# Attention in front of two feed-forward layers: scores of the first two pairs regrouped, score banks in two tiles, selectors made pair by pair

## The chip, the cores and the metric

The kernel runs on one core of one Trainium2 chip. Its engines work at the same time and wait for one another by semaphores: TensorE (PE in the profile, with its weight loads as PEld), VectorE (DVE), ScalarE (ACT), GpSimd (POOL), and SyncE (SP), which here only issues DMAs. The metric is the time on the device in microseconds (us), from launch to end. Three runs of the kernel before took 990.05, 990.08 and 991.07 us, median 990.08.

## The reference

Three stages follow one another; the data are float32.

```python
scores = scale * np.matmul(q, k.transpose(0, 1, 3, 2))          # 4 x 8 heads, 576 x 576, head size 64
cum = np.cumsum(np.log(np.clip(f, 0.0001, 1.0)), axis=-1)
scores = np.where(causal, -1e9, scores + cum[:, :, :, None] - cum[:, :, None, :])
attn = np.exp(scores - np.max(scores, axis=-1, keepdims=True))
x = np.matmul(attn / (np.sum(attn, axis=-1, keepdims=True) + 1e-09), v)
h = x @ w_in;  x = (h * np.cos(h)) @ w_out                      # layer one: 2304 x 512 -> 2048 -> 512
g = x @ w_gate; x = (g / (1 + np.exp(-g)) * (x @ w_val)) @ w_out2   # layer two: 512 -> 1536 -> 512
```

## The kernel before

**Pairs and steps.** Attention works on 16 pairs of heads; a pair fills the 128 rows of TensorE with twice 64. For one pair the score matrix falls into five row tiles, written 0 to 4; tile t < 4 has 128 rows and 128 (t + 1) columns for each head, tile 4 holds the last 64 rows of both heads. The steps have one letter and a tile: `S` computes scores on TensorE (`emit_s`, L381), `M` adds the mask and takes the row maximum on VectorE (L415), `E` is the exponential with row sums on ScalarE (L423), `T` transposes on TensorE (L461), `C` copies the transposed tile out of PSUM (L483 and L485: `C10` and `C11` on VectorE, the others on ScalarE), `V` multiplies with v on TensorE (L513), `N` multiplies with the reciprocal sums on VectorE (L522). The reciprocals go their own way: `ra` on GpSimd (L433), `rb` on VectorE (L435), `rt` a transpose on TensorE (L438), `rc` a copy on ScalarE (`row`, L441), `rd` a write to DRAM, `re` and `rf` two reads that spread it over the rows (L451). `q` splits q and k into a rounded high part and a low rest on GpSimd (xqh L111, xql L108); a score is then three products (high x high, low x high, high x low) in fp32r and a fourth one that adds the decay: a selector (sel) times the cumulative logarithms (cs). Pair 0 is not split; its scores are one fp32 product and the decay. `qb` fills for tile 4 block-diagonal tiles (bd, h for high, l for low, s for the selector) from q and from selr, a small input.

**What sets the order.** The string `SCH` (L46) lists the steps of one iteration; `M21@2` in iteration n is step M, tile 2, second head, of pair n - 2. `in_order` (L586) holds each engine to that order. An iteration has parts of pairs n down to n - 5. In the steady state TensorE goes through T20 (end of the string), T40, rt, T30, T10, T11, T00, T01 of one pair, S4 and S1 of the next, V1 and V0 of an older one, then S3, S2, S0 of the pair after.

**Buffers.** All scores lie in one PSUM tile `s` of four banks (L348); `SAT` gives tiles 1 and 3 the first bank of each head, 0, 2 and 4 the second. Everything that TensorE makes else in this stage takes one of four PSUM tiles `t` in turn, ten times in an iteration: T20, T40, rt, T30, T10, T11, T00, T01, V1, V0. Each take waits until the one four places before it is read out. So T10 waits for C20, T11 for C40, T00 for rc, T01 for C30. Filler matmuls (`warm`, L323) keep TensorE going; `WAIT` (L538) puts five of them behind steps of pairs 0 and 1.

**The beginning.** f lands, VectorE clips it, ScalarE takes the logarithm, VectorE sums it up in two halves of 288 columns (L337 to L342). ScalarE makes the selectors of all 16 pairs (sel, L335 and L343).

**Behind attention.** Layer one (L627 on) multiplies with fp32r halves of weights and data: L246 into h, then ScalarE and VectorE make n, r, the sine, gh and gl, and L660 multiplies gh and gl with w_out. Its tiles n, r (pool mp2) and gh, gl (mp3) are laid where attention had its tiles. The sine table of ScalarE is loaded at L606, after the last `E`. The first matmuls of layer one stand between the last transposes and V steps on TensorE.

Of the kernel before, what the change touches and what calls it, by code (L numbers as in the profile page):

```python
# [26 lines left out]
CH = 384  # L27
# [18 lines left out]
SCH = "M21@2 ld@0 M00@2 T40@3 M01@2 rt@3 M30@2 T30@3 re@4 C40@3 C30@3 rc@3 T10@3 M31@2 w6@4 C10@3 w1@3 T11@3 C11@3 T00@3 C00@3 T01@3 E20@2 C01@3 S4@2 S1@2 V1@4 rf@4 E21@2 w2@3 E30@2 w3@3 w4@3 E31@2 q3@1 M40@2 M10@2 wd@2 E00@2 E01@2 q0@0 M11@2 rd@3 V0@4 S3@1 lv@3 E40@2 S2@1 w5@3 E10@2 xk@3 xo@5 E11@2 q1@0 qb@0 S0@1 T20@2 N1@4 ra@2 N0@4 rb@2 M20@1 w7@4 C20@2 q2@0"  # L46
# [44 lines left out]
def body(ctx: ExitStack, tc: tile.TileContext, qk, v, f, w_in, w_out, w_gate, w_val, w_out2, mask_c, ident_c, sel_c, out):  # L91
# [211 lines left out]
    bd = [[ap1.tile([128, 128], F32R, name=f"bd{k}{a}") for a in "hls"] for k in range(2)]  # L303
# [5 lines left out]
    sel = aps.tile([128, NPAIR, 128], F32R, name="sel")  # L309
    POOL.memset(mask[:, 0:384], 0.0)  # L310
    POOL.memset(mask4[:, 0:512], 0.0)
    for b in (bd0, *bd[0], *bd[1]):
        POOL.memset(b.bitcast(F32), 0.0)
# [14 lines left out]
    warm(WARM, ones[:, 0:128], ones[:, 0:512])  # L328
    DVE.memset(hpi, float(np.pi / 2))
    ACT.activation(out=hpi[:, 0:1], in_=ones[:, 0:1], func=AF.Ln)  # L330
    ACT.activation(out=hpi[:, 0:1], in_=ones[:, 0:1], func=AF.Identity, scale=float(np.pi / 2))
    DVE.tensor_scalar(out=lf, in0=lf, scalar1=1e-4, scalar2=1.0, op0=ALU.max, op1=ALU.min)
    ACT.activation(out=lf, in_=lf, func=AF.Ln)
    for k in range(2):
        ACT.copy(out=sel[:, k], in_=selr[:, k:k + 1].to_broadcast([128, 128]))  # L335
    for a, b in ((0, S // 2), (S // 2, S)):
        DVE.tensor_tensor_scan(out=cum[:, a:b], data0=ones[:, a:b], data1=lf[:, a:b], initial=cum[:, a - 1:a] if a else 0.0,  # L337
                               op0=ALU.mult, op1=ALU.add)
        hi = lc[:, S + a:S + b]
        DVE.tensor_copy(hi.bitcast(F32R), cum[:, a:b])  # L340

        DVE.scalar_tensor_tensor(out=cs[:, a:b], in0=hi, scalar=selr[:, NPAIR:NPAIR + 1], in1=cum[:, a:b], op0=ALU.mult, op1=ALU.add)  # L342
    ACT.copy(out=sel[:, 2:], in_=selr[:, 2:NPAIR, None].to_broadcast([128, NPAIR - 2, 128]))  # L343

    for t in P4s:
        DVE.memset(t[:, S:], 0.0)

    sall = ps_s.tile([128, 2, 2, 512], F32, name="s")  # L348

    SAT = {0: (1, 384), 1: (0, 0), 2: (1, 0), 3: (0, 0)}  # L350
# [3 lines left out]
    def emit_q(i, k):  # L354

        if k == 0:
            xq[i] = [aps.tile([128, 2, S], F32R, tag=a, name=a, bufs=2) for a in ("xqh", "xql")]
        (h, l), x = xq[i], raws[i]
        if k % 2 == 0:
            pool_round(h[:, k // 2], x[:, k // 2])  # L360
        else:
            subtract(POOL, l[:, k // 2], x[:, k // 2], h[:, k // 2])
# [18 lines left out]
    def emit_s(i, t):  # L381
        p = s_parts(i)
        if t < 4:
            q0, ext, _ = QT[t]
            bank, lo = SAT[t]
            o = sall[:, :, bank, lo:lo + ext]
            for m, (x, y) in enumerate(p):
                for e in range(2):
                    b = slice(64 * e, 64 * e + 64)
                    PE.matmul(o[:, e], lhsT=x[b, 0, q0:q0 + 128], rhs=y[b, 1, :ext], start=(m == 0), stop=False)  # L390
            for e in range(2):
                b = slice(64 * e, 64 * e + 64)
# [83 lines left out]
    def emit_c(i, g, e):  # L476
# [61 lines left out]
    WAIT = {("S0", 0): 1, ("S1", 0): 2, ("S1", 1): 2}  # L538

    def op(o, i):  # L540

        if not 0 <= i < NPAIR:
            return
        k, e = o[0], int(o[-1]) if o[-1] in "01" else 0
# [5 lines left out]
        elif k == "S":  # L550
            emit_s(i, int(o[1]))
# [489 lines left out]
```

## Time and profile before

| | |
|---|---|
| median of three runs | 990.08 us |
| time of the profiled execution | 988.04 us |
| its span, first to last instruction | 986.3 us |
| TensorE busy | 973.1 us, 99% of the span |
| VectorE, ScalarE, GpSimd busy | 721.9, 495.2, 476.7 us |
| granted clock of TensorE, mean | 0.998 of full speed |

The profiled execution took 1.74 us more than its span and 2.04 us less than the median of the runs. A busy share in the profile holds overlapped stretches of matmuls whose ends are modelled, so a TensorE that shows no idle time may still lose some; weight loads (PEld) show such small gaps. From about 190 us to the end the kernel is in layers one and two.

### The profile page before, as it was taken

What the parts mean: (1) busy time and instruction counts of PE and PEld (TensorE: products, weight loads), DVE (VectorE), ACT (ScalarE), POOL (GpSimd) and SP (SyncE); (2) the same over time, 40 slices, a digit from 0 to 9 for tenths busy, and PEclk for the clock granted to TensorE, in tenths of its full rate; (3) what the DMA queues carried; (4) which work ended last, traced back from release to release, by engine and by line L of the source; (5) the groups of instructions that cost most, each with busy time, mean ns of one, the idle gap of its engine ahead of it and who ended that gap; (6) DMA issues with size and microseconds to landing.
All of it is one profiled execution on the core that took longest, in us unless ns stands there. A gap on an engine that the chain in (4) does not pass through costs nothing.

```text
span 986.3 us, 18039 instructions
## 1 busy us (share of the span) xinstructions
PE 973.1 (99%) x6458; PEld 930.6 (94%) x6458; DVE 721.9 (73%) x1297; ACT 495.2 (50%) x1112; POOL 476.7 (48%) x531
## 2 busy tenths in 40 slices
PE   8999999899999999999999999999999999999998
PEld 5787877799999999999999999999999999999998
DVE  5888888587788878778785636756768585977874
ACT  5878788455545556556554532323224132443432
POOL 6787875442238678677593004455445455300000
PEclk9999999999999999999999999999999999999999
DMA  4666665433547877769767773325941329954331
GB/s 159 205 187 202 214 182 174 137 107 118 167 150 232 263 224 246 245 210 289 245 198 244 251 272 113 95 82 186 345 128 49 117 73 393 334 161 144 117 105 43
DMA packets 108697, 182.61 MB, mean 185 GB/s; under 512 B 8880, under 2 KB 72256, under 8 KB 108608
## 3 DMA queue, kind: packets, MB, share of 16 engines
q1 hardware_dynamic: 108608, 181.46, 56.8%
q8 instruction: 51, 0.84, 0.4%
q14 instruction: 38, 0.31, 0.1%
HBM read 118.43 MB, written 62.99 MB: 184 GB/s over the span
## 4 chain that ended last, share of the span: by engine, by line
PE 93%; ACT 4%; DMA 1%; issue 1%; DVE 0%; ACTq 0%
PE h L246 20%; PE t L660 19%; PE b L844 11%; PE c L844 8%; PE a L844 8%; PE b L903 6%; PE c L903 4%; PE a L903 4%; PE t L513 4%; PE s L390 3%; ACT pt L485 3%; PE t L461 2%; PE t L663 2%; PE s L399 2%; ACT P L423 1%; PE s L393 1%
## 5 line engine op out<-in xcount | busy, mean ns | idle before, releaser
L246 PE MATMUL h<-xh,w 128*128 128x384 f32 x768 | 149.5, 335 | 0.0
L660 PE MATMUL t<-gh,w 128*128 128x384 f32 x704 | 136.3, 334 | 2.0 <-ACT gh L645 2.0
L246 PEld LDWEIGHTS h<-xh,w 128*128 128x128 f32 x768 | 134.4, 188 | 0.4 <-POOL w L108 0.2
L815 POOL TENSOR_TENSOR s<-u,s 128x384 f32<-128x384 f32 x36 | 41.3, 1147 | 184.1 <-ACT s L814 171.4
L660 PEld LDWEIGHTS t<-gh,w 128*128 128x128 f32 x704 | 123.3, 188 | 2.3 <-ACT gh L645 2.3
L844 PE MATMUL b<-c,wu 128*128 128x384 f32 x648 | 121.1, 334 | 0.0
L637 ACT ACTIVATE n<-h 128x384 int32<-128x384 f32 x96 | 47.1, 491 | 144.9 <-PE h L246 134.0
L639 DVE SCALAR_TENSOR_TENSOR r<-h,n 128x384 f32<-128x384 f32 x96 | 53.4, 556 | 86.7 <-ACT n L637 86.4
L844 PEld LDWEIGHTS b<-c,wu 128*128 128x128 f32 x648 | 113.1, 188 | 0.1
L246 PE MATMUL h<-xl,w 128*128 128x384 f32 x384 | 82.0, 334 | 0.0
L844 PE MATMUL c<-c,wu 128*128 128x384 f32 x432 | 80.7, 334 | 0.0
L844 PE MATMUL a<-c,wu 128*128 128x384 f32 x432 | 80.7, 334 | 0.0
L725 DVE TENSOR_TENSOR u<-b,p 128x768 f32<-128x768 f32 (+1 forms) x54 | 41.9, 777 | 50.0 <-PE b L844 30.0
L844 PEld LDWEIGHTS a<-c,wu 128*128 128x128 f32 x432 | 75.4, 188 | 0.0
L844 PEld LDWEIGHTS c<-c,wu 128*128 128x128 f32 x432 | 75.4, 188 | 0.0
L660 PE MATMUL t<-gl,w 128*128 128x384 f32 x352 | 75.2, 334 | 0.0
L108 POOL TENSOR_TENSOR w<-ta,w 128x512 fp32r<-128x512 f32 x32 | 45.3, 1415 | 58.1 <-ACT w L183 30.1
L423 ACT ACTIVATE P<-P,mx 128x384 f32<-128x384 f32 (+3 forms) x128 | 70.6, 556 | 1.7 <-DVE mx L415 1.7
L246 PEld LDWEIGHTS h<-xl,w 128*128 128x128 f32 x384 | 67.9, 188 | 0.0
L641 ACT ACTIVATE r<-r,hpi 128x384 f32<-128x384 f32 x96 | 59.5, 620 | 12.7 <-DVE r L639 11.7
L169 DVE SCALAR_TENSOR_TENSOR ta<-wraw,ta 128x512 int32<-128x512 int32 x68 | 65.4, 961 | 0.4
L903 PE MATMUL b<-wu,c 128*128 128x256 f32 x486 | 62.8, 283 | 0.6 <-issue 0.6
(150 smaller groups left out, 2125.5 us busy)
## 6 DMA issues: line engine op xcount, KB each, us to landing
wu<-wu SPq DMA_DIRECT2D x63, 512.0 KB, 4.9
wraw<-in_w_out_dram SPq DMA_DIRECT2D x28, 512.0 KB, 4.1
wu<-hi SPq DMA_DIRECT2D x54, 256.0 KB, 3.5
gd<-g SPq DMA_DIRECT2D x72, 192.0 KB, 2.3
gt<-gd SPq DMA_DIRECT2D x36, 384.0 KB, 4.4
raw<-in_qk_dram SPq DMA_DIRECT2D x16, 576.0 KB, 5.3
wu<-sums SPq DMA_DIRECT2D x36, 256.0 KB, 3.6
xb<-x SPq DMA_DIRECT2D x24, 384.0 KB, 8.1
```

Source lines behind the costliest of these rows:

```text
L108: eng.tensor_tensor(out=o, in0=a, in1=b.bitcast(F32), op=ALU.subtract)
L169: DVE.scalar_tensor_tensor(out=ta, in0=hi, scalar=-(1 << 30), in1=ta, op0=ALU.bitwise_and, op1=ALU.bitwise_or)
L246: PE.matmul(ps, lhsT=w[:, a, 128 * kk:128 * kk + 128], rhs=b[:, kk], start=(n == 0), stop=(n == 3 * KD - 1))
L423: ACT.activation(out=o, in_=o, func=AF.Exp, scale=-1.0, bias=mxt[p % 8][:, t:t + 1], accum_out=smt[p // 2 % 3][:, c:c + 1])
L637: ACT.activation(out=n, in_=h, func=AF.Copy, scale=INV2PI, bias=0.25)
L639: DVE.scalar_tensor_tensor(out=r, in0=h, scalar=INV2PI, in1=n, op0=ALU.mult, op1=ALU.subtract)
L641: ACT.activation(out=r, in_=r, func=AF.Sin, bias=hpi, scale=float(2 * np.pi))
L660: PE.matmul(acc[m][:, :CH], lhsT=wo[:, q, 128 * m:128 * m + 128], rhs=x, start=(j == a and n == 0), stop=False)
L725: (e or DVE).tensor_tensor(out=o, in0=a, in1=b, op=op)
L815: e.tensor_tensor(out=s, in0=C[:, 0], in1=s, op=ALU.mult)
L844: PE.matmul(o[:, mem], lhsT=wu[q, i][1][:, mem, x, 128 * kt:128 * kt + 128], rhs=cmb[i][:, y, kt], start=bool(s and n == 0), stop=(n == 5) ...
L903: PE.matmul(ot, lhsT=cmb[i][:, x, q], rhs=wu[NQ + q // 2, i][1][:, q % 2, y], start=bool(s and n == 0), stop=(n == 3 * NQ - 1), skip_group ...
```

## The change

- **Pairs 0 and 1.** Pair 1 takes its tiles 0, 2 and 3 from the raw q and k in one fp32 product, as pair 0 does; its tiles 1 and 4 stay split in three. Pair 0 computes tile 1 right after tile 3, into two tiles `t`, and tile 4 last; its M40 comes after M10 and M11. Two `warm` matmuls remain of five.
- **Score banks.** `s` becomes two tiles, sA (tiles 0, 2, 4) and sB (1, 3). In the string, S2 and S0 now stand before S3; pair 1 alone keeps S3, S2, S0.
- **Order of the transposes.** rt stands before T40 on TensorE, and the copy rc right after C20 on ScalarE. The copies of tails (`tails`) take both heads in one instruction.
- **Selectors.** sel for 16 pairs goes. GpSimd fills, for each pair, one of three tiles of 128 x 256 (two instructions of 64 x 128, zeros in the middle), from which tiles 0 to 3 and tile 4 take their selector. bd holds h and l in one tile, so that one instruction fills both: four small instructions a pair in place of six. xqh and xql become one tile xq.
- **The beginning.** The logarithms go in halves of 384 and 192 columns through clip, logarithm, sum and rounding; the table of the exponential is loaded right behind the logarithms.
- **Sine table and layer one.** The sine table is loaded after the last C01. mp2 and mp3 are made after the tiles of the second chunk (xpool2) and of the sums (pp), and with `reuse_waits="tile"`.

```diff
-SCH = "M21@2 ld@0 M00@2 T40@3 M01@2 rt@3 ... C40@3 C30@3 rc@3 T10@3 ... S3@1 lv@3 E40@2 S2@1 w5@3 ... S0@1 T20@2 N1@4 ra@2 N0@4 rb@2 M20@1 w7@4 C20@2 q2@0"
+SCH = "M21@2 ld@0 M00@2 rt@3 M01@2 T40@3 ... C20@3 rc@3 C40@3 C30@3 T10@3 ... S2@1 lv@3 E40@2 S0@1 w5@3 ... S3@1 T20@2 N1@4 ra@2 N0@4 rb@2 M20@1 w7@4 q2@0"
...
+    bd = [ap1.tile([128, 2, 128], F32R, name=f"bd{k}") for k in range(2)]
+    sels = [ap1.tile([128, 256], F32R, name=f"sel{k}") for k in range(3)]
...
-    for k in range(2):
-        ACT.copy(out=sel[:, k], in_=selr[:, k:k + 1].to_broadcast([128, 128]))
...
+    for c in halves:
+        DVE.tensor_scalar(out=lf[:, c], in0=lf[:, c], scalar1=1e-4, scalar2=1.0, op0=ALU.max, op1=ALU.min)
+        ACT.activation(out=lf[:, c], in_=lf[:, c], func=AF.Ln)
+    ACT.activation(out=sinp, in_=ones[:, 0:1], func=AF.Exp)
...
-    sall = ps_s.tile([128, 2, 2, 512], F32, name="s")
+    sA, sB = (ps_s.tile([128, 2, 512], F32, name=n) for n in ("sA", "sB"))
...
     def emit_b(i):
         q = slice(512, S)
+        s = sels[i % 3]
         for e in range(2):
             b = slice(64 * e, 64 * e + 64)
-            pool_round(bd[i % 2][2][b, b], selr[b, i:i + 1].to_broadcast([64, 64]))
+            pool_round(s[b, 128 * e:128 * e + 128], selr[b, i:i + 1].to_broadcast([64, 128]))
+        for e in range(2):
+            b = slice(64 * e, 64 * e + 64)
             if i:
-                for o, x in zip(bd[i % 2], xq[i]):
-                    pool_round(o[b, b], x[b, 0, q].bitcast(F32))
+                pool_round(bd[i % 2][b, :, b], xq[i][b, :, 0, q].bitcast(F32))
...
+        if i > 1 or i == 1 and t in (1, 4):
+            xh, xl = xq[i][:, 0], xq[i][:, 1]
+            h, l = bd[i % 2][:, 0], bd[i % 2][:, 1]
+            p = (xh, xh, h), (xl, xh, l), (xh, xl, h)
+        else:
+            p = (raws[i], raws[i], bd0),
...
-    WAIT = {("S0", 0): 1, ("S1", 0): 2, ("S1", 1): 2}
+    WAIT = {("S3", 0): 2}
...
+        if i == 0:
+            o = {"M40": "M10", "M10": "M11", "M11": "M40"}.get(o, o)
+        elif i == 1:
+            o = {"S2": "S3", "S0": "S2", "S3": "S0"}.get(o, o)
...
-                    if len(after_e) == 9:
-                        ACT.activation(out=sinp, in_=hpi, func=AF.Sin)
+            if n - int(off) == NPAIR - 1 and o == "C01":
+                ACT.activation(out=sinp, in_=hpi, func=AF.Sin)
...
-    mp2 = lctx.enter_context(tc.tile_pool(name="mp2", bufs=1))
-    mp3 = lctx.enter_context(tc.tile_pool(name="mp3", bufs=3))
     xpools[1] = lctx.enter_context(tc.tile_pool(name="xpool2", bufs=1))
     pp = lctx.enter_context(tc.tile_pool(name="pp", bufs=1))
+    mp2 = lctx.enter_context(tc.tile_pool(name="mp2", bufs=1, reuse_waits="tile"))
+    mp3 = lctx.enter_context(tc.tile_pool(name="mp3", bufs=3, reuse_waits="tile"))
```

On TensorE at the start, before: raw is q and k of the pair, cs the cumulative logarithms, L326 a filler; x2 is one matmul for each head.

```order
L390 MATMUL s<-raw 128x512 [waits DMAHW1_49]
L390 MATMUL s<-raw 128x512
L393 MATMUL s<-cs,sel 128x512 [waits DVE_49,Activation_49]
L393 MATMUL s<-cs,sel 128x512
L390 MATMUL s<-raw 128x384 x2
L393 MATMUL s<-cs,sel 128x384 x2
L390 MATMUL s<-raw 128x128 x2
L393 MATMUL s<-cs,sel 128x128 x2
L326 MATMUL t<-mask,ident 128x448 [waits DMAHW6_49,DMAHW3_49,Pool_49]
L399 MATMUL s<-raw,bd_121 128x288 [waits DVE_49,Pool_49]
```

The same place on TensorE in the changed kernel:

```order
L400 MATMUL sA<-raw 128x384 [waits DMAHW1_49]
L400 MATMUL sA<-raw 128x384
L403 MATMUL sA<-cs,sel_117 128x384 [waits DVE_49,Pool_49]
L403 MATMUL sA<-cs,sel_117 128x384 [waits Pool_49]
L400 MATMUL sA<-raw 128x128 x2
L403 MATMUL sA<-cs,sel_117 128x128 x2
L400 MATMUL sB<-raw 128x512 x2
L403 MATMUL sB<-cs,sel_117 128x512 [waits DVE_49]
L403 MATMUL sB<-cs,sel_117 128x512
L400 MATMUL t<-raw 128x256 x2
L403 MATMUL t<-cs,sel_117 128x256 x2
...
L408 MATMUL sA<-raw,bd_120 128x288 [waits DVE_49,Pool_49]
```

The tile of 384 columns moved ahead of the one of 512, the one of 256 moved ahead of tile 4 (L408, before L399), and the selector is waited for on GpSimd and not on ScalarE.

On ScalarE, the copies of one pair behind its last exponentials, before (128x2x256 is C20, the two of 3x64 are C40, then C30 with two tails, row is the copy rc, L161 a step of the weights):

```order
L485 COPY pt<-t 128x2x256 [waits PE_49]
L485 COPY pt<-t 128x3x64 [waits PE_49]
L485 COPY pt<-t 128x3x64
L485 COPY pt<-t 128x2x128 [waits PE_49]
L485 COPY pt<-t 128x2x64 x2
L441 COPY row<-t 9x128
L161 ACTIVATE ta<-wraw 128x512 [waits DMAHW0_49]
```

The same copies in the changed kernel:

```order
L493 COPY pt<-t 128x2x256 [waits PE_49]
L449 COPY row<-t 9x128 [waits PE_49]
L493 COPY pt<-t 128x2x3x64 [waits PE_49]
L493 COPY pt<-t 128x2x128 [waits PE_49]
L493 COPY pt<-t 128x2x2x64
L161 ACTIVATE ta<-wraw 128x512 [waits DMAHW0_49]
```

The copy of the reciprocals moved from the sixth place behind C20 to the first, and six copies of tiles became four. On TensorE its transpose (rc_174, before rc_176) moved ahead of T40, whose tile is Q. Before:

```order
L461 MATMUL t<-ident,P_110 128x128 [waits Activation_49]
L461 MATMUL t<-ident,Q_113 128x128 [waits PE_49,Activation_49]
L461 MATMUL t<-ident,Q_113 128x128 x2
L438 MATMUL t<-ident,rc_176 9x128 [waits DVE_49,PE_49]
L461 MATMUL t<-ident,P_109 128x128 [waits PE_49]
```

and in the changed kernel:

```order
L469 MATMUL t<-ident,P_110 128x128 [waits Activation_49]
L446 MATMUL t<-ident,rc_174 9x128 [waits DVE_49]
L469 MATMUL t<-ident,Q_113 128x128 [waits PE_49,Activation_49]
L469 MATMUL t<-ident,Q_113 128x128 x2
L469 MATMUL t<-ident,P_109 128x128 [waits PE_49]
```

With this the tiles `t` are taken in the order T20, rt, T40, T30, T10, T11, T00, T01, so that T11 waits for rc and T00 for C40.

## Rows read from the trace of the kernel before

**Rows 1.** Busy time by stretch: engines' us (instructions), granted clock, DMA share, GB/s.
```profile
0.00:20.00 20.00, 15.24 (x62) 8.31 (x63) 8.51 (x30) 11.19 (x26) 13.48 (x37) 0.91 0.56 194
```

**Rows 2.** Waits from 20 to 160 us: us in total, times, longest.
```profile
PEld t L461 <- ACT pt L485: 4.4, 14, 0.4
```

**Rows 3.** Timeline of one pair's transposes: start, us, engine, line [idle before].
```profile
163.32 1.65 ACT L485 COPY pt<-t 128x512 f32<-128x512 f32 x6 [1.64 <-PE t L461]
163.45 0.27 PE L438 MATMUL t<-ident,rc 128*9 128x128 f32 x1
164.80 0.25 ACT L441 COPY row<-t 9x128 f32<-9x128 f32 x1
165.02 0.86 PEld L461 LDWEIGHTS t<-ident,P 128*128 128x128 f32 x8 [0.31 <-ACT pt L485]
165.87 0.51 PE L399 MATMUL s<-xqh,bd1h 128*128 128x288 f32 x2
167.77 2.93 PE L513 MATMUL t<-pt,vt 128*64 128x320 f32 x28
```

**Rows 4.** Timeline of the beginning.
```profile
7.97 0.50 PE L393 MATMUL s<-cs,sel 64*128 64x512 f32 x2 [1.19 <-DVE cs L342]
12.55 1.93 PE L399 MATMUL s<-raw,bd 128*128 128x288 f32 x4 [2.03 <-DVE mx L415]
17.01 0.24 POOL L111 TENSOR_SCALAR bd0l<-xql 64x64 fp32r<-64x64 f32 x1
19.27 0.25 POOL L433 TENSOR_SCALAR rc<-sm 128x9 f32<-128x9 f32 x1 [2.02 <-ACT P L423]
25.43 1.77 PE L326 MATMUL t<-mask,ident 128*128 128x448 f32 x4
```

**Rows 5.** Busy time by stretch, behind the wait at 12.55 us (columns as in Rows 1).
```profile
13.00:14.00 1.00, 1.00 (x5) 0.71 (x3) 0.00 (x0) 1.00 (x6) 1.00 (x2) 0.50 0.00 0
15.00:16.00 1.00, 1.00 (x6) 0.74 (x6) 0.00 (x0) 0.00 (x0) 1.00 (x3) 0.50 0.92 355
```

**Rows 6.** Groups by form on GpSimd, 0 to 160 us: busy us, mean ns.
```profile
L108 POOL TENSOR_TENSOR xql<-raw,xqh 128x576 fp32r<-128x576 f32 x30 | 42.5, 1416 | 1.4
L111 POOL TENSOR_SCALAR xqh<-raw 128x576 fp32r<-128x576 f32 x30 | 20.6, 687 | 25.6 <-PE s L390 25.3
L111 POOL TENSOR_SCALAR bd1s<-selr 64x64 fp32r<-64x64 f32 x16 | 6.9, 434 | 0.5
L111 POOL TENSOR_SCALAR bd1h<-xqh 64x64 fp32r<-64x64 f32 x16 | 3.8, 239 | 0.5
```

**Rows 7.** Timeline from the end of S1 of pair 1.
```profile
25.48 0.67 POOL L111 TENSOR_SCALAR xqh<-raw 128x576 fp32r<-128x576 f32 x1 [3.71 <-PE s L390]
29.72 0.24 POOL L433 TENSOR_SCALAR rc<-sm 128x9 f32<-128x9 f32 x1
34.74 2.93 PE L513 MATMUL t<-pt,vt 128*64 128x320 f32 x28
```

**Rows 8.** Timeline of the end of attention.
```profile
171.92 1.28 ACT L606 ACT_TABLE_LOAD   x1
171.99 0.24 POOL L433 TENSOR_SCALAR rc<-sm 128x9 f32<-128x9 f32 x1 [4.91 <-ACT P L423]
172.63 0.27 PE L438 MATMUL t<-ident,rc 128*9 128x128 f32 x1 [0.66 <-DVE rc L435]
176.02 2.27 PE L513 MATMUL t<-pt,vt 128*64 128x320 f32 x20
187.57 0.49 ACT L637 ACTIVATE n<-h 128x384 int32<-128x384 f32 x1 [10.81 <-DMA x<-xp]
190.47 1.66 PE L660 MATMUL t<-gh,w 128*128 128x384 f32 x8 [1.99 <-ACT gh L645]
```

**Rows 9.** Chain that ended last: the last write of attention's result.
```profile
185.11 2.36 DMA x<-xp
```

More of the change, by code (lines that the diff above doesn't have):

```diff
@@ L45 @@
 CPD = ("10", "11")
-SCH = "M21@2 ld@0 M00@2 T40@3 M01@2 rt@3 M30@2 T30@3 re@4 C40@3 C30@3 rc@3 T10@3 M31@2 w6@4 C10@3 w1@3 T11@3 C11@3 T00@3 C00@3 T01@3 E20@2 C01@3 S4@2 S1@2 V1@4 rf@4 E21@2 w2@3 E30@2 w3@3 w4@3 E31@2 q3@1 M40@2 M10@2 wd@2 E00@2 E01@2 q0@0 M11@2 rd@3 V0@4 S3@1 lv@3 E40@2 S2@1 w5@3 E10@2 xk@3 xo@5 E11@2 q1@0 qb@0 S0@1 T20@2 N1@4 ra@2 N0@4 rb@2 M20@1 w7@4 C20@2 q2@0"
+SCH = "M21@2 ld@0 M00@2 rt@3 M01@2 T40@3 M30@2 T30@3 re@4 C20@3 rc@3 C40@3 C30@3 T10@3 M31@2 w6@4 C10@3 w1@3 T11@3 C11@3 T00@3 C00@3 T01@3 E20@2 C01@3 S4@2 S1@2 V1@4 rf@4 E21@2 w2@3 E30@2 w3@3 w4@3 E31@2 q3@1 M40@2 M10@2 wd@2 E00@2 E01@2 q0@0 M11@2 rd@3 V0@4 S2@1 lv@3 E40@2 S0@1 w5@3 E10@2 xk@3 xo@5 E11@2 q1@0 qb@0 S3@1 T20@2 N1@4 ra@2 N0@4 rb@2 M20@1 w7@4 q2@0"
 JS = 8
@@ L308, in body @@
     selr = aps.tile([128, NPAIR + 1], F32, name="selr")
-    sel = aps.tile([128, NPAIR, 128], F32R, name="sel")
     POOL.memset(mask[:, 0:384], 0.0)
     POOL.memset(mask4[:, 0:512], 0.0)
-    for b in (bd0, *bd[0], *bd[1]):
+    for b in (*sels, bd0, *bd):
         POOL.memset(b.bitcast(F32), 0.0)
@@ L356, in emit_q @@
         if k == 0:
[L357 to L358 removed]
+            xq[i] = aps.tile([128, 2, 2, S], F32R, tag="xq", name="xq", bufs=2)
+        h, l, x = xq[i][:, 0, k // 2], xq[i][:, 1, k // 2], raws[i][:, k // 2]
         if k % 2 == 0:
[L360 removed]
+            pool_round(h, x)
         else:
[L362 removed]
@@ L375, in emit_b, with s_place @@
+        for e in range(2):
+            b = slice(64 * e, 64 * e + 64)
             if i:
-                for o, x in zip(bd[i % 2], xq[i]):
-                    pool_round(o[b, b], x[b, 0, q].bitcast(F32))
+                pool_round(bd[i % 2][b, :, b], xq[i][b, :, 0, q].bitcast(F32))
             else:
                 pool_round(bd0[b, b], raws[i][b, 0, q])
-    def emit_s(i, t):
-        p = s_parts(i)
+    s10 = []
+    def s_place(i, t):
+        if i == 0 and t == 1:
+            if not s10:
+                s10.extend(ps_t.tile([128, 512], F32, tag="t", name="t") for _ in range(2))
+            return [x[:, :256] for x in s10]
+        x, lo = SAT[t]
+        return [x[:, e, lo:lo + QT[t][1]] for e in range(2)]
@@ L383, in emit_s @@
+    def emit_s(i, t):
+        s = sels[i % 3]
+        if i > 1 or i == 1 and t in (1, 4):
[4 more added lines that the diff above has]
+            p = (raws[i], raws[i], bd0),
         if t < 4:
             q0, ext, _ = QT[t]
-            bank, lo = SAT[t]
-            o = sall[:, :, bank, lo:lo + ext]
-            for m, (x, y) in enumerate(p):
+            o = s_place(i, t)
+            for m, (x, y, _) in enumerate(p):
@@ L489, in tails @@
             d = PJ[js[1]] + KW[js[1]] - 64 - a
-            for e in range(2):
-                copy(o[:, e, a:a + d * (n - 1) + 64].rearrange("p (j q) -> p j q", q=64)[:, ::d // 64], x[:, :128 * n].rearrange("p (j e q) -> p j e q", j=n, e=2)[:, :, e])
+            copy(o[:, :, a:a + d * (n - 1) + 64].rearrange("p e (j q) -> p e j q", q=64)[:, :, ::d // 64], x[:, :128 * n].rearrange("p (j e q) -> p e j q", j=n, e=2))
         if g < 2:
@@ L550, in op @@
         elif k == "S":
-            emit_s(i, int(o[1]))
+            if i or o != "S1":
+                emit_s(i, int(o[1]))
+            if not i and o == "S3":
+                emit_s(i, 1)
             warm(WAIT.get((o, i), 0), ident, mask[:, 0:448])
```

47 lines of the change are left out of this document (17 added, 30 removed).

## The prediction, on record before the changed kernel ran

> **What bounds the kernel now.** I read busy time by stretch first, then the waits, then the timeline where they lie. TensorE is the bound: it is 99% busy over the span, and from 190 us to the end it does not wait, so whatever attention saves arrives whole at the end. Most of what it loses lies in three places. In the first 20 us it is busy for 15.24 [rows 1]. In every pair the weight load of T00 waits about 0.31 us for a copy on ScalarE: 4.4 us in 14 pairs [rows 2], and one case in the timeline, at 165.02, where the copy of the reciprocals, begun at 164.80, has just ended [rows 3]. That loss is hidden in the matmul's own busy time. At the end of attention TensorE waits for the reciprocals, then for copies queued behind a table load, then 1.99 us for the first gh [rows 8].
>
> The period of a pair comes from two starts of V, 34.74 and 167.77, 13 pairs apart: 10.23 us [rows 3, 7].
>
> **The transposes (order of rt and rc, tails).** T00 takes the tile that rt filled, and its copy is the last of seven on ScalarE: 163.32 to 165.05 [rows 3]. In the new order T00 waits for C40 and T11 for rc, which stands second. Even if the merged copies saved nothing, the same work ends at 165.05 at the latest, and then only T01 asks for its last piece. Between 163.45 and 165.87 TensorE does rt and 18 transposes, so without the stall one takes (2.42 - 0.31) / 19 = 0.11 us. T01 begins four transposes behind T00 (164.71 without the stall), at 165.15. So the 0.31 us goes, and nothing is late behind it. rt now comes three transposes (0.33 us) earlier. It can, if the reciprocal is there; that is GpSimd's chain, below. The pairs 2 to 14, 13 of them: 13 x 0.31 = 4.0 us.
>
> **Selectors and bd on GpSimd, in the steady state.** The chain that sets M20 and rt starts when S1 ends: two roundings and rests of q and k, the small fills, ra. From 25.48 to 29.72 it is 4.24 us [rows 7], of which 0.69 + 1.42 = 2.1 us are the big ones [rows 6]. Six fills become four. The trace has no fill of 64 x 128. Its price lies between 0.24 us (64 x 64) and 0.69 us (128 x 576), with 0.43 us for the first fill of a group, the mean that holds its delays [rows 6]. I take 0.30, nearest to the small ones. The chain is then some 0.5 us shorter, 3.75 us, and recip and rt stand at 4.15 us after S1. TensorE comes to rt later than that: the period less the way from rt to V (167.77 - 163.45 = 4.32 us [rows 3]) is 5.9 us, less the 0.33 us of T40. The cover is about 1.4 us, so the steady state pays nothing for the selectors.
>
> The Trainium skill speaks against this part: by "SBUF — State Buffer", section "SBUF: two separate sides", VectorE and GpSimd hold a shared pair of ports exclusively for a whole instruction, and the other one blocks. The 434 ns of a selector fill beside 239 ns of the same shape [rows 6] agree with that. By it every fill could cost 0.69 us; the sum would not change, since the chain stays inside its cover.
>
> **The beginning, to the end of S1 of pair 1 (25.43 us [rows 4]).** Before, the first decay product waits until 7.97 us for cs, tile 4 waits 2.03 us more (12.55) for the mask steps of one bank, the clock is at half behind that [rows 5], and ra of pair 0 comes at 19.27, after a wait of 2.02 us for ScalarE's exponentials. GpSimd had ended its own list at 17.25 [rows 4]. In the new order cs has 384 columns about 0.5 us earlier than it had 288 + 288, M20 starts directly behind cs, and tile 4 waits only for tiles 2 and 0. I put the exponentials of pair 0 three to four us earlier, at 15.5. Then GpSimd's own list decides: it has three small instructions less (0.7 us) and six of double width (0.3 us more): ra at 16.9, 2.4 us earlier than now. Bounds: 15.9 (fills at 0.24, nothing delayed) and 19.3 (six at 0.69).
>
> TensorE is ahead of that. Tile 4 of pair 0 starts some two us earlier than at 12.55 and ends its mask step about where it now starts; the raw tiles of pair 1 (no split needed) and T20 are done some 1.9 us behind that, by about 14.4. Then TensorE waits some 2.8 us at rt, which now stands before T40. From ra: 0.4 us to rt, then rt and the 21 transposes of T40 to T01, 2.4 us, then S4 and S1, 167.77 - 165.87 = 1.9 us [rows 3]: 16.9 + 4.7 = 21.6 at full clock. The row behind the wait of 2.03 us shows 0.50 of the clock (1.2 in place of 2.4 GHz) for three rows of 1 us, of which the first and last stand in [rows 5]; behind a wait of 2.8 us I expect the same. Three us at half cost 1.5 us at most, and part of them fall into the wait itself. I charge 1.0: 22.6. The gain is 2.8 us; at full clock it would be 3.8, with the late fills 0.4.
>
> The Trainium skill has the rule: "TensorE: Matmul & The Clock Gate", section "What's actually happening", says that an idle TensorE falls to half its clock and climbs back under sustained work. The rows agree with it (0.50 behind the wait). By the rule the gain here is 2.8 us; if the clock stayed high it would be 3.8.
>
> **The next pair (to 34.74).** It has no V yet, so it is as long as GpSimd's chain. Before it took 34.74 - 25.43 = 9.31 us, with 1.77 us of filler matmuls that covered the chain [rows 4, 7]. The filler goes and the wait shows in its place: S1 to rt 4.15 us, T40 to T01 2.4, S4 and S1 1.9: 8.5 us. The gain is 0.8, not the 1.77 of the filler.
>
> **Table load, mp2, mp3 (from ra of pair 15, 171.99, to the first L660, 190.47: 18.48 us [rows 8]).** ra itself hangs on ScalarE's last exponential and keeps its place behind S1. rt is 0.64 us behind it. Then rt and 21 transposes, 2.4 us, with C20 done long before, since the load of 1.28 us [rows 8] is now behind C01: V begins 3.05 us after ra, in place of 176.02 - 171.99 = 4.03. That is 1.0 us. rt before T40 costs 0.33 us of it already, since TensorE waits there with T40 undone. The second part: n waited until 187.57 for attention's last write to DRAM, since it lay on attention's tiles. In the new place n lies on tiles that are long dead, and so do r, gh and gl; n waits for h alone. What still waits for the write is VectorE's gate for the second chunk (L137), which stands in front of the product that gives gh. It is due 0.6 us (N0) + 2.36 us (the write [rows 9]) + about 1.3 us (gate, product, gh) = 4.3 us behind the last V. TensorE has 30 matmuls of L246 there, at nearly 0.2 us (eight in 1.66 us [rows 8]): 5 us or more. So the 1.99 us go. Together 3.0 us.
>
> **Edits that cost or bring nothing.** Raw products for pair 1: I take one fp32 product to last as long as the three split ones; pair 0 shows it only at a disturbed beginning, so I bound it at 0.2 us each way for the three tiles. The split in two score tiles: S2 first only means that M20 has its tile earlier; it waits for ra's reciprocal anyway. Three tiles of selectors: the third is free long before it is filled.
>
> **The sum.** 2.8 + 0.8 + 4.0 + 3.0 = 10.6 us off the profiled execution's 988.04 us: 977.4. The median of the runs was 2.04 us above that execution, so against 990.08 us the forecast is 979.5 us.
>
> **Rivals.**
> - *The stall of the transposes moves* to T11 (rc waits for rt) or T01, and 4.0 us stay: 983.5 us. For it: T10, T11, T00 and T01 each come within 0.1 to 0.3 us of their copies. Against it: the list of copies is no longer than before. Chance 0.14.
> - *The beginning gives back its gain*: fills at 0.69 us and half a clock for longer. 2.8 + 0.8 falls to about 0.5: 982.6 us. For it: the wait of 2.8 us at rt, longer than any shown. Chance 0.12.
> - *gh stays late*, since L137 still waits for the write and stands before the product in VectorE's order: 2.0 us stay, 981.5 us. Against it: 0.7 us of cover. Chance 0.07.
> - *More*: no fall of the clock, and ScalarE's two spared copies count: 978.2 us. Chance 0.08.
> - *Slower: GpSimd becomes the bound.* If the four fills cost as much as a rest of q (1.42 us [rows 6]), the chain is 2.1 + 5.7 + 0.6 = 8.4 us against the 5.6 us until rt, and each of 14 pairs waits 2.8 us: 39 us lost, 29 us net, about 1008 us. It begins to cost from (5.6 - 2.7) / 4 = 0.72 us a fill and outweighs the gains of 10.6 us from 0.9 us. No fill in the rows is above 0.69. Chance 0.03.
>
> My forecast has the remaining 0.56. Its own range is 978 to 981.5 us. A measurement of this kernel tells a change from none at about 0.2%, 2 us; every case but the slower one is well beyond that. With some chance for what I did not see: faster 0.92, same 0.03, slower 0.05. The range from 977.0 to 984.2 us takes in the cases of more and of 983.5 and leaves out less than 2 in 10.
>
> **What would show it.** The wait of PEld at L461 for ScalarE in the steady state gone and the period of a pair at 9.9 us; ra of pair 0 near 16.9 us with a wait of TensorE at rt before it and a lower clock behind it; S1 of pair 1 ending near 22.6; V of pair 14 about 3 us behind the last ra; no wait at the first gh. I am wrong if the period stays above 10.1 us, if TensorE waits at rt in every pair, or if layer one waits where attention did not.

## The result, and the profile after

The changed kernel takes 981.05 us (median of 4 runs, 979.8 to 981.92) against 990.07 us: a ratio of 0.991, 95% interval 0.989 to 0.993. It is faster, by 9.0 us; 979.5 was forecast, within 977.0 to 984.2. Measured again on another occasion it took 982.21 us against 989.1 us, 0.993 (0.992 to 0.994). The profiled execution took 981.92 us with a span of 980.1 us, 6.2 us less than the span of before.

The transposes first. The waits from 20 to 160 us, those of TensorE and its weight loads (us in total, times, longest):

```profile
PEld t L469 <- issue: 5.1, 14, 0.4
PEld sA L400 <- issue: 2.5, 13, 0.5
PEld t L446 <- DVE rc L443: 1.7, 1, 1.7
PE t L446 <- DVE rc L443: 1.5, 1, 1.5
```

The line that answers to [rows 2] is gone: no weight load of a transpose waits for a copy on ScalarE. The first line is another place, T20, whose weight loads now stand behind the long products of S3; TensorE's own work has no gap there, and the run with the order alone (below) has the same period without this line. (L469 is the old L461, L446 the old L438, L441 and L443 the old L433 and L435, L520 the old L513, L669 the old L660.) The timeline of the last pair's transposes, to be held beside [rows 3]:

```profile
156.65 0.09 PEld L446 LDWEIGHTS t<-ident,rc 128*9 128x9 f32 x1
157.59 1.51 PEld L469 LDWEIGHTS t<-ident,P 128*128 128x128 f32 x14
161.01 0.47 PEld L520 LDWEIGHTS t<-pt,vt 128*64 128x64 f32 x6
```

Fourteen transposes run in one group. V starts at 32.57 and at 161.01 us, 13 pairs apart: a period of 9.88 us in place of 10.23, 4.6 us in all.

The beginning, to be held beside [rows 4, 5, 7]: first its timeline.

```profile
17.13 0.25 POOL L441 TENSOR_SCALAR rc<-sm 128x9 f32<-128x9 f32 x1
17.68 0.09 PEld L446 LDWEIGHTS t<-ident,rc 128*9 128x9 f32 x1 [2.62 <-DVE rc L443]
21.54 0.95 PEld L408 LDWEIGHTS sA<-xq,bd 128*128 128x128 f32 x6
23.64 0.67 POOL L111 TENSOR_SCALAR xq<-raw 128x576 fp32r<-128x576 f32 x1 [4.00 <-PE sB L400]
24.39 1.98 POOL L108 TENSOR_TENSOR xq<-raw,xq 128x576 fp32r<-128x576 f32 x1
28.33 0.09 PEld L446 LDWEIGHTS t<-ident,rc 128*9 128x9 f32 x1 [1.69 <-DVE rc L443]
32.57 1.54 PEld L520 LDWEIGHTS t<-pt,vt 128*64 128x64 f32 x14
```

Then two stretches of it (columns as in [rows 1]: the granted clock stands ahead of the DMA share).

```profile
18.00:19.00 1.00, 1.00 (x9) 1.00 (x8) 1.00 (x9) 0.73 (x2) 0.92 (x2) 0.68 0.00 0
20.00:21.00 1.00, 1.00 (x7) 1.00 (x6) 1.00 (x4) 0.23 (x1) 0.00 (x0) 0.50 1.07 192
```

TensorE waits 2.62 us at the rt of pair 0, runs at 0.50 of its clock behind that (1.2 of 2.4 GHz), and needs 3.9 us from rt to S4. V comes 2.2 us earlier than at 34.74.

The end of attention, to be held beside [rows 8, 9]:

```profile
165.35 0.24 POOL L441 TENSOR_SCALAR rc<-sm 128x9 f32<-128x9 f32 x1 [4.49 <-ACT P L431]
168.41 2.27 PE L520 MATMUL t<-pt,vt 128*64 128x320 f32 x20
175.21 0.81 SPq L145 DMA_DIRECT2D wraw<-in_w_in_dram  x2
176.07 0.43 SPq L534 DMA_DIRECT2D x<-xp  x1
176.74 0.49 ACT L646 ACTIVATE n<-h 128x384 int32<-128x384 f32 x1 [6.04 <-PE h L246]
181.36 0.14 DVE L137 CAST xl<-gs 1x1 fp32r<-1x1 f32 x1 [3.55 <-DMA x<-xp]
182.01 0.48 ACT L654 CAST gh<-h 128x384 fp32r<-128x384 f32 x1 [2.64 <-DVE h L652]
182.54 1.66 PE L669 MATMUL t<-gh,w 128*128 128x384 f32 x8 [1.68 <-ACT gh L654]
```

V stands 3.06 us behind ra, and n waits for TensorE, no longer for the write. But the write is issued at 176.07, behind two weight loads of 512 KB. The chain that ended last shows how long it took:

```profile
176.07 5.17 DMA x<-xp
```

VectorE's gate at L137 waits for it (a cast of one element that lets the load of the second chunk go when attention's result is written). VectorE's product that gives gh (L652) stands behind the gate, and so the first product of layer one on TensorE still waits 1.68 us. It comes 7.9 us earlier than in before. From there to the end this execution takes 797.6 us, 1.8 more than the 795.8 of before; that difference is the subject of three runs below.

### The profile page after: what moved, and what is told of

Its sections match the earlier page's. It is cut to its first block, busy times and chain, and to the rows that moved or that the text cites. A ratio compares the mean times of both kernels' runs of the same rounds, so it can differ in the third digit from the quotient of the medians.

```text
span 980.1 us, 17944 instructions
## 1 busy us (share of the span) xinstructions
PE 966.5 (99%) x6446; PEld 927.6 (95%) x6446; DVE 723.5 (74%) x1298; ACT 491.1 (50%) x1079; POOL 474.4 (48%) x500
## 4 chain that ended last, share of the span: by engine, by line
PE 92%; DMA 2%; ACT 2%; POOL 1%; DVE 1%; issue 1%; SPq 0%; DVEq 0%; POOLq 0%; ACTq 0%
PE h L246 19%; PE t L669 18%; PE b L853 11%; PE c L853 8%; PE a L853 7%; PE b L912 6%; PE t L469 4%; PE c L912 4%; PE a L912 4%; PE t L520 4%; PE sB L400 2%; PE t L672 2%; PE sA L408 1%; PE sA L400 1%; ACT P L431 1%; DMA wraw<-in_w_out_dram 1%
## 5 line engine op out<-in xcount | busy, mean ns | idle before, releaser
L669 PE MATMUL t<-gh,w 128*128 128x384 f32 x704 | 136.9, 335 | 2.0 <-ACT gh L654 2.0
L669 PEld LDWEIGHTS t<-gh,w 128*128 128x128 f32 x704 | 123.0, 188 | 3.6 <-ACT gh L654 3.0
L669 PE MATMUL t<-gl,w 128*128 128x384 f32 x352 | 75.2, 334 | 0.0
```

Of the source, the lines that this page charges most:

```text
L669: PE.matmul(acc[m][:, :CH], lhsT=wo[:, q, 128 * m:128 * m + 128], rhs=x, start=(j == a and n == 0), stop=False)
```

## The experiments

All times are medians, each with its ratio to before and the 95% interval. Differences to the changed kernel are against its second measurement, 982.21 us. The runs below come from three occasions, on which the kernel before had medians of 989.1, 989.1 and 989.8 us, so a difference of 1 us or less says nothing.

**The changed kernel again, and the kernel before again** (no edit).

> The changed kernel once more, as the yardstick for the other kernels on the same chip, and as a second trace. Between the first product of layer one (182.54 us) and the end its first trace spends 797.6 us, the kernel before 795.8. Theory A (chance): the 1.8 us are weight loads that landed late in that one execution, so this trace shows another sum of waits in layer one, and the time comes out at 979 to 981 us. Theory B (the change costs layers one and two 1.8 us for good, since attention ends 8 us earlier on the same stream of weights): the same waits at the same places, TensorE's weight loads waiting for ScalarE near 441 and 508 us, and again 797.5 us from the first product to the end.

982.21 us, 0.993 (0.9917 to 0.9943). V at 32.59 us, first product at 182.68, so 797.8 us from there to the end, with a wait of 0.5 us for ScalarE near 508 us again, but none near 441. By this trace theory B; the next one bears on it too.

> The kernel before once more, for a second trace. From the first product of layer one to the end its first trace spends 795.8 us; eight traces of kernels with the change spend 796.7 to 798.4. Theory A (the change costs layers one and two about 1.8 us): 795.5 to 796.2 us again. Theory B (the first trace of before was at the fast end of its own scatter: its 988.04 us lie 1.1 us under the median of 29 later runs, 989.1): 797 us or more.

One run, 990.74 us, with a span of 989.0. The first and the second product of layer one, and a stretch of 1 us between them (its columns: stretch, length, TensorE's busy time, granted clock, DMA share, GB/s):

```profile
190.99 2.14 PE L660 MATMUL t<-gh,w 128*128 128x384 f32 x8 [1.94 <-ACT gh L645]
196.83 1.55 PE L660 MATMUL t<-gh,w 128*128 128x384 f32 x8
192.00:193.00 1.00, 1.00 (x5) 0.50 1.02 384
```

From the first product it takes 798.0 us: the number of theory B. But 1.6 us of it are TensorE's clock: the second product starts 5.84 us behind the first, at 0.50 of the clock from 192 to 195 us, where the first trace of before needs 4.27 us at full clock (190.47 to 194.74) and the changed kernel as much (182.54 to 186.81). From the second product on, which leaves this out, the four traces with n, r, gh and gl in their old place (both of before, and two of the runs below) take 791.6 to 792.3 us, the ten with the new place 791.8 to 794.1, on average 793.1. So the 1.8 us between the first two traces are scatter in part, and the change may cost layers one and two some 1 us; the two ranges overlap, and the runs do not settle it. Between this trace of before and the first of after, V comes 2.7 us earlier (35.30 to 32.57), the 13 periods take 4.6 less, the stretch from the last V of that count to the first product 1.1 less, and the layers 0.4: together the 8.9 us between the spans.

**One part alone, and that part undone.** In the kernel before, and back again in the kernel after:

```diff
-T40@3 M01@2 rt@3 M30@2 T30@3 re@4 C40@3 C30@3 rc@3 ... C20@2
+rt@3 M01@2 T40@3 M30@2 T30@3 re@4 C20@3 rc@3 C40@3 C30@3 ...
```

> The kernel before with one part of the change alone: the places of rt, T40, rc and C20 in the order. In before the reciprocal is there 1.0 us ahead of TensorE's rt, which now comes 0.33 us earlier. Theory A (the order alone ends the wait of T00): no wait of T00's weight load for ScalarE, period 9.9 to 9.95 us in place of 10.23, 3.6 to 4.3 us less in the steady state, up to 0.7 us of it lost at the first and last rt: 985 to 986 us. Rival (it needs the merged copies, or GpSimd's six fills are then too late for rt): period above 10.1, or a wait at rt in every pair, and 1.5 us less at most.

985.68 us, 0.9961 (0.9947 to 0.9975). Two starts of V:

```profile
33.05 2.69 PEld L513 LDWEIGHTS t<-pt,vt 128*64 128x64 f32 x28
161.49 2.69 PEld L513 LDWEIGHTS t<-pt,vt 128*64 128x64 f32 x28
```

The period is (161.49 - 33.05) / 13 = 9.88 us: the order alone brings all of it, with split tails and six fills. V comes 1.7 us earlier than in before (34.74), but 1.6 us of that is the clock, which stays at 1.00 behind the wait at 12.5 us where [rows 5] has 0.50. At the first product of layer one TensorE waits 3.0 us here.

> The changed kernel with rt, T40, rc and C20 in their old places in the order; all else, the merged copies too, stays new. Theory A (the place of rc and C20 among ScalarE's copies is what ended the wait of T00): the weight load of T00 waits again for ScalarE, the period of a pair goes from 9.88 back to about 10.2 us, and the time rises by 4 us, less up to 1 us that rt behind T40 gives back at the beginning and at the end. Rival (the merged copies of the tails are what ended it): the period stays below 9.95 and the time within 1 us of the changed kernel's.

984.58 us, 0.9958 (0.9944 to 0.9971), 2.4 us above the changed kernel. The waits from 20 to 160 us:

```profile
PEld t L469 <- ACT pt L493: 3.2, 13, 0.3
```

V at 31.26 and 163.25 us, a period of 10.15: 13 x 0.27 = 3.5 us come back, less 1.3 us in the beginning of this execution, where the clock did not fall. Theory A.

**The tails split again** in the changed kernel.

```diff
-            copy(o[:, :, a:a + d * (n - 1) + 64].rearrange("p e (j q) -> p e j q", q=64)[:, :, ::d // 64], x[:, :128 * n].rearrange("p (j e q) -> p e j q", j=n, e=2))
+            for e in range(2):
+                copy(o[:, e, a:a + d * (n - 1) + 64].rearrange("p (j q) -> p j q", q=64)[:, ::d // 64], x[:, :128 * n].rearrange("p (j e q) -> p j e q", j=n, e=2)[:, :, e])
```

> The changed kernel with the copies of the tails in two instructions each, as before; the order stays new. Theory A (the place of rc and C20 ended the wait of T00, the merged copies at most add to it): the period stays between 9.88 and 9.95 us, the time within 1 us of the changed kernel's. Rival (ScalarE has no room for the two copies more): weight loads of T00 or T01 wait for ScalarE again, period 10.0 us or more, time 2 us or more above.

981.82 us, 0.9925 (0.9912 to 0.9937); period (161.98 - 32.94) / 13 = 9.93 us. Theory A: the merged copies are worth 0.6 us at most, and the time does not show it.

**The gate one step later.**

```diff
-... c == 0 and j == 1 and 1 not in loaded:
+... c == 0 and j == 2 and 1 not in loaded:
```

> The load of the second chunk, with its gate on VectorE, one step of layer one later, so that the gate stands behind the first product and not in front of it. Theory A (the gate waits for attention's last write and holds the product): the first gh is ready some 3 us earlier, the wait of 1.7 us (weight load 2.0 us) at the first product of L669 is gone, and the time falls by 1.5 to 2.0 us against the changed kernel. Rival (gh would be late without the gate too, by ScalarE's sine or its table): the wait stays at 1 us or more, and the time stays.

979.01 us, 0.9895 (0.988 to 0.9911), 3.2 us below the changed kernel. The timeline:

```profile
177.66 0.57 DVE L652 TENSOR_TENSOR h<-h,r 128x384 f32<-128x384 f32 x1 [0.68 <-ACT r L650]
178.43 0.48 ACT L654 CAST gh<-h 128x384 fp32r<-128x384 f32 x1
179.86 1.55 PE L669 MATMUL t<-gh,w 128*128 128x384 f32 x8
180.46 0.14 DVE L137 CAST xl<-gs 1x1 fp32r<-1x1 f32 x1 [0.88 <-DMA x<-xp]
```

VectorE's product (L652) stands ahead of the gate, gh is there at 178.91, 0.95 us before it is wanted, and the wait is gone: theory A. Counted from the last V (171.68 to 179.86, against 172.51 to 182.54) that is 1.85 us. The rest of the 3.2 us is of the size of what the clock gives (below): the mean clock is 1.000 in three of the four executions, and in this trace it did not fall at the beginning.

**The write ahead of the weight loads** (an order between the two on the DMA queue, no wait added).

```diff
         SP.dma_start(out=raw, in_=srcs[kind][j])
+        if lastx:
+            tc.add_manual_dep(nc.cur_bb.bb.instructions[-1], lastx[0].name, mybir.DependencyInfo(
+                mybir.DependencyClass.NoSync, mybir.DependencyReason.DATA), reason="order")
...
+    lastx.append([x for x in nc.cur_bb.bb.instructions if x.engine == nc.sync.engine][-1])
```

> The changed kernel with attention's last write issued ahead of the two 512 KB weight loads of layer one, which stood before it in the DMA queue. Theory A (the write takes 5.3 us and not 2.4 us because its packets queue behind those loads): the gate stands at 178.5 to 179 us in place of 181.36, the first gh is some 2.5 us earlier, the wait of 1.7 us at the first product is gone, time 1.5 us less. Rival (the write is slow by itself in that place, or by the loads that follow it): the gate stays at 180.5 us or later and 1 us of wait stays.

980.03 us, 0.9905 (0.989 to 0.992). The timeline (line numbers are four or five higher here):

```profile
175.70 2.32 SPq L538 DMA_DIRECT2D x<-xp  x2
177.25 0.42 DVE L533 TENSOR_TENSOR xp<-t,rs 128x256 f32<-128x256 f32 x1 [0.16 <-PE t L524]
178.13 0.87 SPq L146 DMA_DIRECT2D wraw<-in_w_in_dram  x2
180.20 0.14 DVE L137 CAST xl<-gs 1x1 fp32r<-1x1 f32 x1 [0.64 <-DMA x<-xp]
182.44 1.55 PE L674 MATMUL t<-gh,w 128*128 128x384 f32 x8
```

From the end of the last normalization the gate stands 2.5 us behind (177.67 to 180.20), against 5.45 in the changed kernel (175.91 to 181.36), and no wait is left at the first product. Theory A: the loads ahead of it are what made the write slow. The first product comes late here only because attention began late: rt of pair 0 at 18.65, then half the clock.

**The old place of n, r, gh and gl.**

```diff
+    mp2 = lctx.enter_context(tc.tile_pool(name="mp2", bufs=1))
+    mp3 = lctx.enter_context(tc.tile_pool(name="mp3", bufs=3))
     xpools[1] = lctx.enter_context(tc.tile_pool(name="xpool2", bufs=1))
     pp = lctx.enter_context(tc.tile_pool(name="pp", bufs=1))
-    mp2 = lctx.enter_context(tc.tile_pool(name="mp2", bufs=1, reuse_waits="tile"))
-    mp3 = lctx.enter_context(tc.tile_pool(name="mp3", bufs=3, reuse_waits="tile"))
```

> The changed kernel with the tiles n, r, gh and gl (pools mp2 and mp3) back in their old place, opened before the second chunk's pool and without waits tile by tile; all else new. Two questions. At the first product of layer one, theory A (the new place is what frees n from attention's last write): n waits for the write again, the first gh comes some 2 us later than in the changed kernel, first product near 184.5 us. Rival: n was free anyway, 182.6 us. In the rest of layers one and two, theory A2 (the new place also moves the second chunk's tiles, and its loads then take longer): from the first product to the end 795.8 us as before, in place of the 797.6 to 797.8 us of three traces with the new place; then the time is about that of the changed kernel. Rival: 797.5 us again, and the time is 2 us above the changed kernel's.

984.81 us, 0.995 (0.9937 to 0.9962), 2.6 us above the changed kernel. The timeline:

```profile
182.54 0.49 ACT L646 ACTIVATE n<-h 128x384 int32<-128x384 f32 x1 [10.68 <-DMA x<-xp]
185.43 2.33 PE L669 MATMUL t<-gh,w 128*128 128x384 f32 x8 [3.43 <-ACT gh L654]
```

n waits for the write again, and the first product waits 3.43 us, 1.75 more: theory A. The run takes back the place and the waits tile by tile together, so which of the two frees n is not shown. The layers behind took 798.2 us, the rival's number; but here, too, the clock is at 0.50 behind the wait (187 to 189 us), and the second product starts 5.85 us behind the first. Without these 1.6 us they take 796.6, from the second product on 792.3. A2 stays open.

**Every small fill twice.**

```diff
+            for _ in range(1 + (i > 3)):
                 pool_round(s[b, ...], selr[b, i:i + 1].to_broadcast([64, 128]))
```

(and the same around the fill of bd)

> Each of the four small fills of a pair (selector halves, bd halves) is issued twice from pair 4 on, with the same result. The changed kernel's trace has them at 0.33 to 0.55 us each, 1.3 to 1.7 us a pair, and the sum ra waits 0.4 us for ScalarE behind them; TensorE takes the reciprocals 0.6 us after they are there. Theory A (the chain has 0.4 + 0.6 us of room): GpSimd's second set of 1.3 to 1.7 us makes TensorE wait 0.3 to 0.7 us at rt in each of 12 pairs, 4 to 8 us more. Theory of the prediction (room of 1.4 us): 0 to 0.3 us a pair, up to 3 us more. Rival (GpSimd's chain is not near the path): no change.

991.93 us, 1.0028 (1.0017 to 1.0039): 9.7 us above the changed kernel. The timeline of one pair (L443 is ra here, L448 rt):

```profile
110.32 1.73 POOL L111 TENSOR_SCALAR sel<-selr 64x128 fp32r<-64x128 f32 x4
112.11 1.40 POOL L111 TENSOR_SCALAR bd<-xq 64x128 fp32r<-64x128 f32 x4
113.59 0.24 POOL L443 TENSOR_SCALAR rc<-sm 128x9 f32<-128x9 f32 x1
114.20 0.09 PEld L448 LDWEIGHTS t<-ident,rc 128*9 128x9 f32 x1 [0.83 <-PE t L471]
```

The four fills take 3.13 us where they took 1.74 (the row is below, under the hardware), and TensorE waits 0.83 us at rt in each pair from the second doubled one on (the profile puts the weight load's wait down to PE, the matmul's own to VectorE's reciprocal). The room is 1.39 - 0.83 = 0.56 us: neither the 1.4 us of the prediction nor the 1.0 us of theory A, whose 4 to 8 us were exceeded.

**The small fills behind ra.**

```diff
-... q1@0 qb@0 S3@1 T20@2 N1@4 ra@2 N0@4 ...
+... q1@0 S3@1 T20@2 N1@4 ra@2 qb@0 N0@4 ...
```

> The small fills of the selectors and bd behind the sum of the row sums (ra) in GpSimd's order, in every pair. Theory A (GpSimd's own list sets the end of the wait at the first rt): ra of pair 0 at 15.3 us in place of 17.13, rt of pair 0 at 15.9 in place of 17.68, rt of pair 1 some 1.3 us less behind S1, V starts at 29.5 to 30.5 us in place of 32.57; in the steady state nothing (there ra already waits for ScalarE's exponentials), so 2 to 3 us less in all. Rival (VectorE or ScalarE sets rt as much): ra earlier by less than 0.5 us, no change of the time. Rival on the other side: the late fills of bd hold back the scores of tile 4, and each pair grows.

979.2 us, 0.9901 (0.9888 to 0.9915), 3.0 us below the changed kernel.

```profile
16.50 0.09 PEld L446 LDWEIGHTS t<-ident,rc 128*9 128x9 f32 x1 [1.66 <-DVE rc L443]
25.54 0.09 PEld L446 LDWEIGHTS t<-ident,rc 128*9 128x9 f32 x1
29.84 2.69 PEld L520 LDWEIGHTS t<-pt,vt 128*64 128x64 f32 x28
```

V starts at 29.84 us, 2.7 us earlier. Of this 1.2 us are the first rt (16.50 in place of 17.68, ra at 15.96): there GpSimd's own list had set the wait, as theory A has it. The other 1.5 us are the clock, which did not fall here: from rt to S4 (18.82) it is 2.3 us in place of 3.9. The next pair became no shorter, and there theory A missed: rt of pair 1 stands 4.7 us behind the end of S1 (20.8 to 25.54) as it did (23.6 to 28.33). Its wait is gone, but TensorE waits 2.0 us ahead of it for the mask of pair 1's tile 4, which VectorE is late with. The price is 0.04 us a pair (period 9.92).

**Fillers in the wait at the first rt.**

```diff
-    WAIT = {("S3", 0): 2}
+    WAIT = {("S3", 0): 2, ("S0", 1): 3}
```

> The changed kernel with three filler matmuls (0.9 us each) of no use in TensorE's wait at the rt of pair 0, 2.6 us long. In the two traces of the changed kernel the granted clock falls to 0.50 behind that wait and S4 of pair 1 starts 3.9 us behind rt; in two other traces it stays at 1.0 and S4 starts 2.3 us behind. Theory A (the idle time lets the clock fall, some executions more, some less): with the filler the clock is 1.0 throughout, S4 of pair 1 starts 2.3 us behind rt, V at 31.6 us in place of 32.57, and the time is that of the executions without a fall, 980 to 981 us, some 1.5 us below the changed kernel's median of 982.2. Rival (the fall comes from something else): 0.50 again behind rt, no gain.

980.81 us, 0.9915 (0.9897 to 0.9933). In this trace the clock is as theory A has it: the stretches of 1 us from 14 to 22 show 1.00, S4 stands 2.4 us behind rt. That the fillers hold it up is not shown: one of the four executions has a mean clock of 0.998 (982.6 us), and with the gate moved the clock stayed up without fillers. Nor is the price settled: rt came at 18.60 here, and V at 32.34, only 0.23 us earlier; the rest of the 1.4 us lies in layers that took 796.1 us.

**Both faster edits together** (gate and small fills).

> The two edits that were faster, together: the small fills behind the sum ra, and the second chunk's load one step later. Theory A (one saves at the beginning, the other at the end of attention, and TensorE has nothing in between to catch up): V starts at 29.8 us, no wait of 1.6 us at the first product of L669, the sum of the two gains: 4.5 to 6 us below the changed kernel, 976 to 978 us. Rival (the earlier end of attention meets the stream of weights earlier and gives a part back in layer one): 978 us or more, with longer waits for ScalarE in layer one.

978.25 us, 0.9888 (0.9873 to 0.9904): the fastest of all, 4.0 us below the changed kernel measured again, less than the sum of the two gains (6.2).

```profile
30.17 2.69 PEld L520 LDWEIGHTS t<-pt,vt 128*64 128x64 f32 x28
178.91 1.55 PE L669 MATMUL t<-gh,w 128*128 128x384 f32 x8
```

V at 30.17, no wait at the first product: theory A's mechanism, just under its size. The time is the rival's, but its reason is not seen, since the layers behind took 797.2 us, within their scatter. The two gains do not add up because some 1.4 us of each was the clock that did not fall, and that can be gained only once.

## Why the prediction was right, and where its steps failed

**Transposes, 4.0 us: right, 4.6 measured** (0.35 us a pair where 0.31 had been read). The order alone ends the wait for ScalarE and brings the whole of it. Neither of the rival's stalls appeared.

**Beginning, 2.8 and 0.8 us: the mechanism right, both terms too large.** S1 of pair 1 ended at 23.6, not 22.6. rt came at 17.68 where ra at 16.9 and 0.4 us had made it 17.3. The half clock was charged at 1.0 us; from rt to S4 it took 3.9 us against 2.3 at full clock (18.04 to 20.36 in the kernel with the late gate): 1.5 us. The next pair took 8.97 us instead of 8.5, since the rest of q cost 1.98 us where 1.42 had been read. That the raw products of pair 1 cost nothing held: its tiles 3, 2 and 0 took 2.4 us (12.24 to 14.64, 0.3 us of it a wait), the split ones of pair 2 2.3 us (23.94 to 26.22). What the score tiles, the raw products, GpSimd's selectors and the halves of the logarithms each gave at the beginning is not separated by any run.

**Selectors at no cost in the steady state: true, but the cover was mis-sized.** The prediction took 1.4 us from GpSimd's list alone. In the changed kernel ra waits for ScalarE's exponentials 0.4 us behind the fills, and TensorE takes the reciprocals some 0.6 us later; doubling the fills showed 0.56 us of room. The slower rival's threshold of 0.72 us a fill would have been (1.74 + 0.56) / 4 = 0.58, and its time was added up wrongly: 29 us above 990.08 are 1019 us, not 1008.

**End of attention, 3.0 us: 1.3 measured from ra to the first product (17.19 in place of 18.48 us); this step failed.** Its first half held (V 3.06 us behind ra, 3.05 forecast), and so did n's freedom from the write (putting the tiles back cost 1.75 us more wait). The failed term is "2.36 us (the write)". The trace of before has the same two weight loads here:

```profile
181.92 0.81 SPq L145 DMA_DIRECT2D wraw<-in_w_in_dram  x2
185.11 0.33 SPq L527 DMA_DIRECT2D x<-xp  x1
```

That write was issued 3.2 us behind them and took 2.36 us. In the changed kernel it comes 9.0 us earlier, but the loads, which wait for GpSimd's weight steps, only 6.7: it is issued 0.9 us behind them (175.21, 176.07) and takes 5.2 us. Two runs lie between: 2.3 us behind the loads it took 3.27 us (old places of rt and rc in the changed kernel), 1.2 us behind them 4.95 (the order alone). In all four it landed 5.5 to 6.2 us behind the issue of the loads, whenever it was issued itself. The 0.7 us of cover went, and the rival "gh stays late" came true for 1.7 of its 2.0 us. The write put first, or the gate behind the product, takes the wait away.

The Trainium skill has the rule that was overlooked: "DMA: Bandwidth & Descriptors", section "Queues, rings and completion order", says that each DMA engine consumes descriptors in ring order. The runs agree: 5.45 us to the gate behind the loads, 2.5 ahead of them.

**The sum.** Terms of 10.6 us became 2.2 to V, 4.6 for 13 periods and 1.2 from there on: 7.9 us to the first product. So 2.7 us of gain were missing, and yet the forecast of 979.5 us came out only 1.5 us below the 981.05 measured. The rest is luck: on the second occasion the gain was 6.9 us and not 9.0, and over all executions of both kernels it is 7.7 (981.7 against 989.4). The trace of before that the sum was made against had no half clock in layer one, the second trace of before had (1.6 us); such falls may be most of the 2.04 us by which the median lay above that trace, but the runs without a trace do not show it.

## What to carry to other kernels

A copy that ends a wait late on its engine may need only another place in the order; measure that edit alone before crediting the ones made with it. The price of a DMA read from a trace holds for what stood ahead of it on its queue then: when other work is moved earlier, ask what it now stands behind. Before you call a chain covered, look at who else its last link waits for. And before you credit an edit with what differs between two traces, hold the granted clock of both side by side.

## What the runs showed of the hardware

**The clock falls in some executions and not in others, at the same place in the program.** Behind 2.4 us without a matmul (15.3 to 17.7 us) the changed kernel's clock fell to 0.50 in both of its traces; with the gate moved, far behind this place, TensorE stood idle longer, from 15.1 to 18.0, and the clock stayed. Its stretches:

```profile
16.00:17.00 1.00, 0.00 (x0) 1.00 0.05 16
17.00:18.00 1.00, 0.00 (x0) 1.00 0.00 0
19.00:20.00 1.00, 1.00 (x11) 1.00 0.02 5
```

(Columns as above.) So the length of the wait alone does not decide it. Nor does the program: the kernel before and its copy with the order alone are the same up to the wait of 2.03 us at 12.5 us, and behind it the clock is at 0.50 in the one [rows 5] and at 1.00 in the other. A fall cost 1.5 us behind rt (3.9 us to S4 in place of 2.3) and 1.6 us behind the first product of layer one. Of ten executions of the changed kernel the four with a mean clock of 1.000 took 980.6 us on average, the six with 0.997 or 0.998 took 982.4; only two of them were traced, so where the others lost it is not shown. Why it fell in the one and not in the other stays open.

**GpSimd and VectorE slow each other.** In the changed kernel, the first line from a stretch in which GpSimd has nothing to do (149.9 to 155.5 us), the others from the steady state:

```profile
152.64 0.69 DVE L169 SCALAR_TENSOR_TENSOR ta<-wraw,ta 128x512 int32<-128x512 int32 x1
113.11 1.30 DVE L169 SCALAR_TENSOR_TENSOR ta<-wraw,ta 128x512 int32<-128x512 int32 x1
113.83 1.09 POOL L111 TENSOR_SCALAR sel<-selr 64x128 fp32r<-64x128 f32 x2
114.98 0.65 POOL L111 TENSOR_SCALAR bd<-xq 64x128 fp32r<-64x128 f32 x2
```

The same weight step takes 0.69 us without GpSimd's work and 1.30 beside it; the pair of selector fills takes 1.09 us beside it, and 0.65 behind it, like the fills of bd, when it is moved behind ra (the run with the small fills moved).
